# Slot products of an attention and soft-MoE kernel in eight wide matmuls, one reciprocal step per batch, and a new order of steps

## Chip, cores and metric

The kernel runs on one core of a Trainium2 chip. The metric is the device time of one execution in microseconds (us); lower is better. All data are float32. The engines are named as the profile names them: PE is TensorE (PEld its weight loads), DVE is VectorE, ACT is ScalarE, POOL is GpSimd, and SP issues the DMAs.

## What is computed

An attention between 512 tokens and 32 states per head, in both directions, feeds a soft mixture of experts over all 4608 rows (8 batches of 512 tokens and 32 states).

```python
# attention: x (8, 8, 512, 64), state (8, 8, 32, 64)
scores = scale * np.matmul(x, state.transpose(0, 1, 3, 2))      # softmax over the 32 states
xread = np.matmul(softmax(scores), state)
scores2 = scale * np.matmul(state, x.transpose(0, 1, 3, 2))     # softmax over the 512 tokens
sread = np.matmul(softmax(scores2), x)
x = concatenate([xread, sread], axis=2)                         # to (4608, 512)
# soft mixture of experts: phi (512, 32), w1 (8, 512, 1024), w2 (8, 1024, 512)
logits = x @ phi
d = np.exp(logits - logits.max(0)); d /= d.sum(0) + 1e-09       # over all rows
slot_input = d.T @ x                                            # 32 slots, 4 per expert
h = np.maximum(slot_input[e] @ w1[e], 0.0)
slot_out[e] = h @ w2[e]
c = np.exp(logits - logits.max(1)); c /= c.sum(1) + 1e-09       # over the 32 slots
return c @ slot_out
```

## The kernel before

The program is a list of small steps. The text `ORDER` names them one after the other, each with its batch, head parity or group, and each step issues its instructions when its turn comes; an engine takes its own instructions in that order and waits for what they need. A `!` behind a copy step puts that copy on DVE, without it the copy is on ACT. The text `HOMES` says by hand which of the 8 PSUM banks (`b`), 11 half buffers (`h`), 5 `big` and 8 `wide` buffers each new tile takes, so a tile also waits until the last user of its buffer is through.

Steps of batch b (h is the parity of the head, 0 or 1): `X` turns x on PE and `xe` copies it out. `S` makes the scores, two PSUM banks of 128x512, a row for each state of four heads. The token side of the softmax: `q` turns a bank with DVE (32x32 blocks), `m1` takes the largest of each 32, `sub` subtracts it on POOL, `x1` is the exponential on ACT, `l1` sums each 32 on DVE, `r1` adds the small constant and takes the reciprocal (two DVE instructions, lines 367 and 368), `mul` multiplies on POOL, and `aT` turns the result back on DVE. The state side: `m2` (DVE), `e2` (ACT, with the row sum), `l2` (two DVE instructions, lines 394 and 395), `E` and `ee` turn and copy the exponentials, `R` multiplies by x, `sr` divides, `srT` and `srTe` turn and copy.

The sums lie in `l1s` and `l2s` beside a column that holds 1e-9, so that one `tensor_reduce` over pairs adds the constant. `r1` runs for each h alone, so `mul.b.0` waits only for half 0.

`G` (line 291) makes the products of phi and the states once: for each of 8 batches and 4 head pairs one matmul with a 128x32 state as weights and a 64 columns wide `phi_bd`, in which POOL has laid phi out with zeros (lines 286 to 289). `Ge` copies the bank to `G_sb` on ACT (line 304). `Lx` multiplies `G_sb` with the turned softmax; this gives the logits without x ever being formed.

For a group of two batches then come the largest logit (`mx`, `mk`, `bm`, `nme`), `dx` (exponential), `dT` and `dTe` (turn and copy), `T` with the turned softmax `A` / `ae`, `tt` (DVE turn), `Px` with the turned states `U` / `Ue`, and `Y`, which adds to the running slot input `y`. `Ls` to `Ys` do the same for the rows of the states (`V` / `Ve` and `D` among them). `Wd`, `We`, `SI` and `SIe` close the softmax over all rows; `SIe` (line 728) writes the slot input `si_m`, on which all of the rest waits.

The rest: `W.hf.e` (line 755) multiplies with w1 into two halves, `hc`, `ht`, `hr` copy, turn and rectify a half into `h_m` (zeroed by `hz` on POOL), `u.c.hf.e` (line 817) multiplies with w2 into the two column halves c, `c` and `s` (lines 823 to 833) sum over the four row blocks, `cm`, `cx`, `cd`, `cb` make the softmax over the slots, `o.k.q` (line 842) makes 128x512 blocks of the output, four banks each, which ACT and DVE copy and SP sends out, and `os` does so for the state rows. For k = 3 each two copies are sent as a DMA of their own (`HALVED`).

SP issues all loads in one fixed order: x, states, phi, then 33.5 MB of weights, each as soon as its buffer is free (`ld`).

Of the kernel before, what the change touches and what calls it, by code (L numbers as in the profile page):

```python
# [32 lines left out]
X.0.0 xe.0.0! X.0.1 xe.0.1! X.0.2 X.0.3 xe.0.3 xe.0.2! S.0 q.0.0 X.1.0 xe.1.0 X.1.1 X.1.3 X.1.2 xe.1.1 m1.0.0  # L33
sub.0.0 m2.0.0 xe.1.3 xe.1.2 q.0.1 m2.0.1 m1.0.1 sub.0.1 x1.0.0 l1.0.0 r1.0.0 e2.0.1 G.0 Ge.0 S.1 q.1.0 X.2.3 E.0.1
mul.0.0 q.1.1 e2.0.0 x1.0.1 ee.0.1 l1.0.1 X.2.0 E.0.0 ee.0.0 X.2.1 X.2.2 m1.1.1 r1.0.1 xe.2.3 m1.1.0 xe.2.1 xe.2.0
sub.1.1 R.0.0 m2.1.0 aT.0.0 l2.0 m2.1.1 R.0.1 xe.2.2 S.2 e2.1.0 sub.1.0 x1.1.0 sr.0 m2.2.0 mul.0.1 aT.0.1 e2.1.1
x1.1.1 X.3.2 l2.1 E.1.0 ee.1.0 X.3.0 A.0.0 xe.3.0 ae.0.0 X.3.1 E.1.1 X.3.3 q.2.0 xe.3.1 srT.0 l1.1.1 q.2.1 ee.1.1
srTe.0 X.4.0 l1.1.0 m1.2.1 sub.2.1 r1.1.1 R.1.0 m2.2.1 xe.3.2 R.1.1 xe.3.3 S.3 sr.1 srT.1 r1.1.0 e2.2.0 E.2.0 e2.2.1
m1.2.0 X.4.2 x1.2.1 srTe.1 m2.3.0 ee.2.0 E.2.1 mul.1.1 aT.1.1 xe.4.0 X.4.1 ee.2.1 m2.3.1 mul.1.0 aT.1.0 sub.2.0
xe.4.1 A.1.1 X.4.3 Lx.0.0 Lx.0.1 l2.2 x1.2.0 Lx.1.0 Lx.1.1 ae.1.1 q.3.0 l1.2.1 ld.0 m1.3.0 sub.3.0 r1.2.1 mul.2.1  # L40
xe.4.3 R.2.0 R.2.1 xe.4.2 S.4 e2.3.0 mx.0 mk.0 sr.2 keep.0 srT.2 x1.3.0 bm.0 srTe.2 q.3.1 e2.3.1 A.0.1 l1.2.0 X.5.0
m1.3.1 sub.3.1 ae.0.1 r1.2.0 xe.5.0 m2.4.0 aT.2.1 X.5.3 xe.5.3 nme.0 X.5.2 q.4.0 mul.2.0 l1.3.0 dx.0 Lu.0 E.3.1
X.5.1 xe.5.2 m1.4.0 xe.5.1 E.3.0 r1.3.0 mul.3.0 A.1.0 sub.4.0 x1.3.1 dT.0 dTe.0 q.4.1 S.5 e2.4.0 U.0 l1.3.1 E.4.0
ae.1.0 T.0 ee.3.1 m1.4.1 ee.3.0 R.3.0 m2.4.1 R.3.1 e2.4.1 aT.2.0 A.2.0 l2.3 X.6.2 r1.3.1 ee.4.0 m2.5.0 mul.3.1
aT.3.0 A.3.0 Ue.0 x1.4.0 sr.3 srT.3 m2.5.1 aT.3.1 e2.5.0 xe.6.2 tt.0 sub.4.1 x1.4.1 X.6.1 E.5.0 Lx.2.0 Lx.2.1 q.5.0
l1.4.1 m1.5.0 sub.5.0 ae.2.0 Lx.3.0 srTe.3 r1.4.1 e2.5.1 l2.4 Lx.3.1 Ls.0 q.5.1 X.6.0 l1.4.0 E.4.1 m1.5.1 keep.1
Lse.0 mx.1 X.6.3 xe.6.1 r1.4.0 l2.5 A.2.1 X.7.1 ae.3.0 xe.6.0 xe.6.3 sub.5.1 S.6 x1.5.0 l1.5.0 A.3.1 q.6.1 ae.2.1
ee.4.1 ee.5.0 q.6.0 E.5.1 Lr.0 msx.0 mul.4.1 ae.3.1 R.4.0 R.5.0 R.4.1 ee.5.1 R.5.1 mk.1 pv.1 m1.6.1 m1.6.0 mul.4.0
m2.6.1 sr.4 x1.5.1 l1.5.1 bm.1 lkp.0 nme.1 xe.7.1 r1.5.0 aT.4.0 X.7.0 dsx.0 srT.4 e2.6.1 xe.7.0 dx.1 X.7.2 m2.6.0
E.6.1 xe.7.2 sub.6.0 aT.4.1 X.7.3 xe.7.3 sr.5 r1.5.1 mul.5.0 mul.5.1 dT.1 e2.6.0 sub.6.1 dTe.1 als.0 Lus.0 S.7 D.0  # L50
aT.5.0 ee.6.1 m2.7.1 aT.5.1 Px.0 V.0 E.6.0 ee.6.0 l2.6 x1.6.0 T.1 Lx.4.0 q.7.0 tt.1 al.0 m1.7.0 e2.7.1 srTe.4 x1.6.1
Ve.0 Lx.4.1 Lx.5.0 m2.7.0 e2.7.0 Lx.5.1 mx.2 R.6.0 R.6.1 srT.5 E.7.1 ee.7.1 A.5.1 E.7.0 sr.6 q.7.1 l1.6.0 m1.7.1
pv.2 mk.2 A.4.1 sub.7.0 srTe.5 ee.7.0 l1.6.1 x1.7.0 sub.7.1 ld.1 ld.2 ld.3 ae.5.1 srT.6 bm.2 nme.2 srTe.6 ae.4.1
r1.6.0 mul.6.0 l1.7.0 l2.7 Px.1 x1.7.1 keep.2 R.7.0 R.7.1 r1.6.1 A.4.0 A.5.0 sr.7 srT.7 dx.2 mul.6.1 srTe.7 ae.4.0
U.1 r1.7.0 Ps.0 Ls.1 Lse.1 l1.7.1 dT.2 dTe.2 aT.6.0 mul.7.0 A.6.0 r1.7.1 aT.6.1 Lr.1 ae.5.0 al.2 Lx.6.0 Lx.6.1 al.1
mul.7.1 aT.7.0 Ue.1 T.2 Lx.7.0 aT.7.1 msx.1 lkp.1! Lx.7.1 tt.2 ae.6.0 mx.3 pv.3! A.7.0 mk.3! Lu.1 als.1 A.6.1 dsx.1
Y.0 bm.3 D.1 Ys.0 nme.3 V.1 ae.7.0 A.7.1 Y.1 dx.3 dT.3 Px.2 Ve.1 ae.6.1! ld.4 ae.7.1! windows Lu.2 Ps.1 Y.2 Ys.1
dTe.3 T.3 Lus.1 al.3 Lu.3 tt.3 Wd Px.3 We Y.3 SI SIe W.0.0 W.0.1 ld.5 ld.6 keep.3! cm.1 hz W.0.2 W.0.3 W.0.4 W.0.5
W.0.6 W.0.7 W.1.0 hc.0 ht.0 cm.0 W.1.1 W.1.2 cm.2 cx.2 hr.0 u.0.0.0 W.1.3 u.0.0.1 W.1.4 u.0.0.2 W.1.5 ld.7 ld.8 ld.9
ld.10 u.0.0.3 ld.11 W.1.6 cx.0 cd.0 u.1.0.0 W.1.7 cx.1 cd.1 u.0.0.4 u.0.0.5 hc.1! ht.1 u.0.0.6 u.0.0.7 hr.1 u.0.1.0  # L60
u.0.1.1 ld.12 u.0.1.2 u.0.1.3 u.0.1.4 ld.13 ld.14 cd.2 cb.2 cb.1 u.0.1.5 u.0.1.6 u.0.1.7 ld.15 u.1.1.0 c.0 s.0
u.1.0.1 cb.0 o.1.0 os.0 o.1.1 o.0.0 o.0.1 u.1.1.1 u.1.0.2 u.1.1.2 u.1.0.3 u.1.1.3 u.1.0.4 u.1.1.4 u.1.0.5 u.1.1.5
# [4 lines left out]
0 1 2 3 4 0 2 3 4 1 0 2 3 4 1  # L67
# [859 lines left out]
```

## Time and profile before

| what | value |
|---|---|
| median of 3 runs | 136.93 us (136.19 to 139.18) |
| the profiled execution's own time | 135.94 us |
| its span, first to last instruction | 134.1 us |
| PE busy | 116.4 us (87%) |
| DVE busy | 89.9 us (67%) |
| ACT busy | 74.5 us (56%) |
| POOL busy | 45.1 us (34%) |
| HBM read, written | 42.53 MB, 8.91 MB |

Times inside the execution count from the start of the span. Busy time is a sum over instructions; the ends of matmuls are modelled, so a PE that reads as busy may still have room.

### The profile page before, as it was taken

The numbers are of one execution on the slowest core, as the hardware profiler recorded it, in microseconds if no ns is written. First come the engines' busy times: TensorE is split into PE (matmuls) and PEld (weight loads), VectorE is DVE, ScalarE is ACT, GpSimd is POOL, SyncE is SP. The second block draws the span as 40 slices with busy tenths as digits, with TensorE's granted clock in tenths as the row PEclk, the third lists the DMA queues.
The fourth block names the chain that finished last, engine by engine and source line by source line (L and its number), as shares of the span: only waits on it lengthen the run. The fifth ranks groups of instructions, "written<-read, shape, count | busy, mean of one in ns | idle before, by whom it ended". The sixth has DMA issues, their size and how long they took to land.

```text
span 134.1 us, 4428 instructions
## 1 busy us (share of the span) xinstructions
PE 116.4 (87%) x1852; PEld 80.1 (60%) x1852; DVE 89.9 (67%) x228; ACT 74.5 (56%) x179; POOL 45.1 (34%) x64
## 2 busy tenths in 40 slices
...
GB/s 115 370 412 452 415 440 401 450 420 432 428 415 445 410 445 398 428 423 447 418 435 406 414 394 345 420 430 442 423 440 392 57 348 434 418 134 338 419 428 147
DMA packets 7220, 51.73 MB, mean 386 GB/s; under 512 B 800, under 2 KB 928, under 8 KB 3488
## 3 DMA queue, kind: packets, MB, share of 16 engines
...
q14 instruction: 6, 0.05, 0.1%
HBM read 42.53 MB, written 8.91 MB: 384 GB/s over the span
## 4 chain that ended last, share of the span: by engine, by line
PE 62%; DVE 19%; issue 5%; DMA 5%; ACT 1%; DVEq 0%; SPq 0%; ACTq 0%
PE h_ps L755 11%; PE o L842 7%; PE xt_ps L320 7%; PE so_ps L817 6%; DMA out_x<-out 5%; PE an_ps L402 4%; PE sc L334 4%; PE sr_ps L427 4%; PE spin L282 3%; DVE nm L383 3%; PE eT_ps L402 3%; DVE aT L377 3%; DVE m L352 3%; DVE q L347 3%; PE lt L457 2%
## 5 line engine op out<-in xcount | busy, mean ns | idle before, releaser
L356 POOL TENSOR_TENSOR q<-q,m 128x512 f32<-128x512 f32 x16 | 16.7, 1048 | 19.5 <-DVE r L367 11.2
L261 ACT ACTIVATE xt<-xt_ps 128x512 f32<-128x512 f32 x29 | 16.5, 619 | 6.9 <-PE xt_ps L320 6.8
L372 POOL TENSOR_TENSOR q<-q,r 128x512 f32<-128x512 f32 x16 | 16.7, 1049 | 6.1 <-DVE r L368 3.3
L854 DVE COPY out<-o 128x512 f32<-128x512 f32 x16 | 10.0, 683 | 12.1 <-PE o L842 12.0
L320 PE MATMUL xt_ps<-ident,x 128*128 128x128 f32 x112 | 16.3, 276 | 0.0
L755 PE MATMUL h_ps<-w,si_m 128*32 128x512 f32 x128 | 15.3, 594 | 0.4 <-DVE si_m L728 0.4
L320 PEld LDWEIGHTS xt_ps<-ident,x 128*128 128x128 f32 x112 | 12.6, 141 | 3.1 <-issue 2.7
L817 PE MATMUL so_ps<-w,h_m 128*32 128x256 f32 x216 | 14.2, 380 | 0.0
L817 PEld LDWEIGHTS so_ps<-w,h_m 128*32 128x32 f32 x216 | 8.2, 110 | 7.2 <-issue 4.3
L258 ACT COPY so_sb<-so_ps 128x256 f32<-128x256 f32 x2 | 0.7, 372 | 19.9 <-PE so_ps L817 14.2
L347 DVE STREAM_TRANSPOSE q<-sc 128x512 f32<-128x512 f32 x16 | 10.9, 693 | 1.2 <-PE sc L334 1.2
L388 ACT ACTIVATE e<-sc,nm 128x512 f32<-128x512 f32 x16 | 11.2, 700 | 0.6 <-DVE nm L383 0.4
L842 PE MATMUL o<-lt_all,so_r 32*128 32x512 f32 x64 | 10.8, 630 | 0.5 <-ACT so_r L258 0.5
L377 DVE STREAM_TRANSPOSE aT<-q 128x512 f32<-128x512 f32 x16 | 11.0, 690 | 0.3 <-PE sc L334 0.2
L853 ACT COPY out<-o 128x512 f32<-128x512 f32 x16 | 8.7, 591 | 3.8 <-PE o L842 3.6
L383 DVE TENSOR_REDUCE nm<-sc 128x1 f32<-128x512 f32 x16 | 10.6, 661 | 0.0
L352 DVE TENSOR_REDUCE m<-q 128x16 f32<-128x512 f32 x16 | 10.6, 665 | 0.0
L363 DVE TENSOR_REDUCE l1s<-q 128x16 f32<-128x512 f32 x16 | 10.4, 649 | 0.0
L359 ACT ACTIVATE q<-q 128x512 f32<-128x512 f32 x16 | 10.2, 634 | 0.2 <-POOL q L356 0.2
L755 PEld LDWEIGHTS h_ps<-w,si_m 128*32 128x32 f32 x128 | 8.6, 110 | 2.6 <-issue 0.8
L334 PE MATMUL sc<-xt,x_b 64*32 64x512 f32 x112 | 9.8, 601 | 0.2 <-ACT xt L261 0.2
L258 ACT COPY eT<-eT_ps 128x512 f32<-128x512 f32 x16 | 9.2, 600 | 1.2 <-PE eT_ps L402 1.2
...
## 6 DMA issues: line engine op xcount, KB each, us to landing
...
```

What stands on the lines that cost most here:

```text
L261: (dve.tensor_scalar_mul if Z["dve"] else act.mul)(out, in_, by)
L320: pe.transpose(p[:, P * j : P * j + P], xg[b, g][:, j, :], ident)
L334: pe.matmul(r[f"sp{h}"][32 * g : 32 * g + 32, :], st_t(b, g)[64 * h : 64 * h + 64, :], r[f"xt{g}"][64 * h : 64 * h + 64, :], start=True, s ...
L347: dve.transpose(r[f"q{h}"], r[f"sp{h}"])
L352: dve.tensor_reduce(out=r[f"m1{h}"], in_=r[f"qv{h}"], axis=AX.X, op=ALU.max)
L356: pool.tensor_tensor(v, v, R[b][f"m1{h}"].broadcast_to([P, 16, NS]), op=ALU.subtract)
L372: pool.tensor_tensor(v, v, R[b][f"r1{h}"].broadcast_to([P, 16, NS]), op=ALU.mult)
L377: dve.transpose(r[f"aT{h}"], r[f"q{h}"])
L383: dve.tensor_reduce(out=r[f"nm2{h}"], in_=r[f"sp{h}"], axis=AX.X, op=ALU.max, negate=True)
L755: pe.matmul(h_ps[hf][32 * kt : 32 * kt + 32, :], si_m[kt // 2][:, 256 * (kt % 2) + 32 * e : 256 * (kt % 2) + 32 * e + 32], wt[1, hf, e, kt ...
L817: pe.matmul(so[c][32 * i : 32 * i + 32, :], h_m[hf][:, 256 * i + 32 * e : 256 * i + 32 * e + 32], wt[2, c, e, 4 * hf + i], start=i0, stop= ...
L842: pe.matmul(o[j], so_r[hf][rows, col : col + 128], lt_all[rows, 4 * q : 4 * q + 4, :].rearrange("p b s -> p (b s)"), start=True, stop=True,)
```

## The change

The products of phi and the states become 8 matmuls of 256 columns: phi is now the weight, 64 rows and 32 columns of it, and the states of all 8 batches are streamed; two banks result, which two DVE transposes turn into `G_sb`, and `phi_bd` goes. `l1s` and `l2s` become one tile `ls` with 34 pairs per batch (two times 16 of the token side, 2 of the state side), and `r1` (twice) and `l2` become one step `rr` of one reduction and one reciprocal over 34 numbers. It stands behind both `l1` and both `e2` of its batch; `mul` and `sr` read their part of it. `ORDER` and `HOMES` are replaced.

```diff
-    l1s = cp.tile([P, 4, 16, 2], F32, name="l1s")
-    l2s = cp.tile([P, 2, 2, 2], F32, name="l2s")
-    pool.memset(l1s, EPS)
-    pool.memset(l2s, EPS)
+    ls = cp.tile([P, 2, 34, 2], F32, name="ls")
+    pool.memset(ls, EPS)
...
-        phi_bd = half("phi_bd")[:, 0 : 8 * NS].rearrange("p (g h n) -> p g h n", g=4, h=2)
-        pool.memset(phi_bd, 0.0)
-        for h in range(2):
-            pool.tensor_copy(phi_bd[64 * h : 64 * h + 64, :, h, :], phi_sb[64 * h : 64 * h + 64])
...
         def G(b):
-            R[0]["gp"] = p = bank([P, B, 2 * NS], "g_ps")
-            for b in range(B):
-                for g in range(4):
+            p = R[0]["gp"] = [bank([P, B * NS], f"g_ps{h}") for h in range(2)]
+            for g in range(4):
+                for h in range(2):
                     pe.matmul(
-                        p[32 * g : 32 * g + 32, b, :],
-                        st_t(b, g),
-                        phi_bd[:, g].rearrange("p h n -> p (h n)"),
+                        p[h][32 * g : 32 * g + 32, :].rearrange("p (q b n) -> p q b n", q=4, b=2),
+                        phi_sb[64 * h : 64 * h + 64, g, :],
+                        stT_sb[64 * h : 64 * h + 64, :, g % 2, g // 2],
...
-            act.copy(G_sb, R[0]["gp"].rearrange("p b (h n) -> p b h n", h=2))
+            for h in range(2):
+                dve.transpose(G_sb[:, h].rearrange("p b n -> p (b n)"), R[0]["gp"][h])
...
-        def r1(b, h):
-            R[b][f"r1{h}"] = t = sm.tile([P, 16, 1], F32, tag=f"r1{h}", name=f"r1_{b}_{h}")
-            dve.tensor_reduce(out=t, in_=l1s[:, 2 * (b % 2) + h], axis=AX.X, op=ALU.add)
+        def rr(b):
+            R[b]["rr"] = t = sm.tile([P, 34, 1], F32, tag="rr", name=f"rr_{b}")
+            dve.tensor_reduce(out=t, in_=ls[:, b % 2], axis=AX.X, op=ALU.add)
             dve.reciprocal(t, t)
...
-        def l2(b):
-            R[b]["l2"] = t = sm.tile([P, 2, 1], F32, tag="l2", name=f"l2_{b}")
-            dve.tensor_reduce(out=t, in_=l2s[:, b % 2], axis=AX.X, op=ALU.add)
-            dve.reciprocal(t, t)
...
-u.1.0.6 u.1.1.6 u.1.0.7 u.1.1.7 c.1 s.1 o.2.0 o.3.0 o.3.1 spin.3 o.2.1 os.1
+u.1.0.6 u.1.1.6 u.1.0.7 u.1.1.7 c.1! s.1! o.3.0 o.3.1 os.1 o.2.0 o.2.1 spin.3
```

On DVE before there are, in the attention, three `xe`, two `ae`, and one each of `keep`, `lkp`, `mk` and `pv`; now three `xe`, three `ae`, two `lkp`, and one each of `srTe`, `dTe` and `Ve`. After the attention DVE had `hc.1`; now it has `hc.0`, `c.0`, `c.1` and `s.1`.

Three places show how the order moves. The first is DVE in batches 2 and 3 (the first number in a name is the batch, the second the half). Before:

```order
L352 TENSOR_REDUCE m_3_0_610<-q_0_605 128x16
L367 TENSOR_REDUCE r_2_1_613<-l1s 128x16
L368 RECIPROCAL r_2_1_613<-r_2_1_613 128x16
L473 TENSOR_REDUCE mx_666<-lt_582 128x1
L438 TENSOR_TENSOR sr_670<-sr_ps_619,l_2_591 128x128
L347 STREAM_TRANSPOSE q_1_679<-sc_1_509 128x512
L363 TENSOR_REDUCE l1s<-q_0_444 128x16
L352 TENSOR_REDUCE m_3_1_694<-q_1_679 128x16
L367 TENSOR_REDUCE r_2_0_698<-l1s 128x16
L368 RECIPROCAL r_2_0_698<-r_2_0_698 128x16
```

Now, for the same batch 2:

```order
L345 TENSOR_REDUCE m_3_0_604<-q_0_594 128x16
L340 STREAM_TRANSPOSE q_1_640<-sc_1_439 128x512
L345 TENSOR_REDUCE m_3_1_642<-q_1_640 128x16
L355 TENSOR_REDUCE ls<-q_0_503 128x16
L255 COPY srT_455<-srT_ps_626 128x4x32
L361 TENSOR_REDUCE rr_664<-ls 128x34
L362 RECIPROCAL rr_664<-rr_664 128x34
L426 TENSOR_TENSOR sr_680<-sr_ps_514,rr_664 128x128
```

Half 1 had its reciprocal three large steps ahead of half 0; now both halves and the state side have theirs in one step, behind the last sum.

The second place is DVE at the end of the attention, from the last group's `nme.3` to `SIe`. Before:

```order
L537 TENSOR_REDUCE nm_all<-bm_ps_1573 128x1
L529 SCALAR_TENSOR_TENSOR y<-y,al_all,px_ps_1388 128x128
L258 COPY an_1549<-an_ps_1_1564 128x16x32
L258 COPY an_1584<-an_ps_1_1586 128x16x32
L529 SCALAR_TENSOR_TENSOR y<-y,al_all,px_ps_1598 128x128
L529 SCALAR_TENSOR_TENSOR y<-y,al_all,ps_ps_1619 128x128
L585 STREAM_TRANSPOSE tt_1650<-t_ps_1628 128x128
L700 TENSOR_SCALAR rl<-l_ps 128x32
L701 RECIPROCAL rl<-rl 128x32
L529 SCALAR_TENSOR_TENSOR y<-y,al_all,px_ps_1654 128x128
L728 TENSOR_TENSOR si_m_1613<-si_ps,rl 128x8x4 x2
L728 TENSOR_TENSOR si_m_1615<-si_ps,rl 128x8x4 x2
```

Now; behind these rows follow three `y`, the two `rl` and the four `si_m`:

```order
L525 TENSOR_REDUCE nm_all<-bm_ps_1464 128x1
L255 COPY an_1421<-an_ps_1_1458 128x16x32
L255 COPY an_1489<-an_ps_0_1467 128x16x32
L255 COPY an_1489<-an_ps_1_1473 128x16x32
L637 TENSOR_REDUCE lr_1494<-lr_1494 128x1
L493 TENSOR_TENSOR nm_all<-lr_1494,nm_all 128x1
L517 SCALAR_TENSOR_TENSOR y<-y,al_all,px_ps_1500 128x128
L573 STREAM_TRANSPOSE tt_1517<-t_ps_1393 128x128
L517 SCALAR_TENSOR_TENSOR y<-y,al_all,ps_ps_1512 128x128
L255 COPY srN_1520<-v_ps_1448 128x512
L658 STREAM_TRANSPOSE D_1525<-ds_1522 128x32
L573 STREAM_TRANSPOSE tt_1570<-t_ps_1527 128x128
```

More of DVE's work stands behind `nme.3` (the row of `nm_all`) than before: the state group's part, a third `an`, a copy of `srN` and a second `tt` have moved there.

The third place is PE between the last product of the first column half (`so_ps` of c = 0) and the first output block. Before:

```order
L817 MATMUL so_ps_1752<-w_1789,h_m 32x256 x4
L817 MATMUL so_ps_1808<-w_1791,h_m 32x256 x4
L832 MATMUL sum_ps_1904<-so_sb_1901,rep 128x256
L817 MATMUL so_ps_1808<-w_1797,h_m 32x256 x4
L842 MATMUL o_0_0_1912<-lt_all,so_r_1903 128x512
```

Now:

```order
L805 MATMUL so_ps_1730<-w_1647,h_m 32x256 x4
L805 MATMUL so_ps_1817<-w_1657,h_m 32x256 x8
L820 MATMUL sum_ps_1827<-so_sb_1813,rep 128x256
L805 MATMUL so_ps_1817<-w_1676,h_m 32x256 x8
L830 MATMUL o_0_0_1840<-lt_all,so_r_1826 128x512
```

In both, `so_sb` is the copy of the first bank. Before, one part of the second half stood between that bank and the sum (its fellow far ahead, in the w1 stage), now two; behind the sum two instead of one.

## Rows read from the trace of the kernel before

**Rows 1.** By stage: stretch, length, busy PE, PEld, DVE, ACT, POOL, clock, DMA, GB/s

```profile
5.30:54.80 49.50, 48.29 (x905) 36.65 (x905) 46.84 (x113) 44.36 (x107) 26.07 (x29) 1.00 1.01 423
54.80:79.30 24.50, 20.56 (x474) 16.75 (x473) 19.55 (x61) 16.21 (x46) 11.00 (x20) 1.00 1.01 422
79.30:102.80 23.50, 23.50 (x280) 15.53 (x280) 11.75 (x33) 1.94 (x4) 7.08 (x7) 1.00 1.01 414
102.80:110.50 7.70, 7.62 (x52) 3.31 (x46) 4.54 (x8) 5.26 (x11) 0.00 (x0) 1.00 0.55 225
...
117.60:124.50 6.90, 5.64 (x39) 2.44 (x39) 4.88 (x8) 4.74 (x10) 0.00 (x0) 1.00 0.57 236
```

**Rows 2.** Chain that ended last: start us, us, what; one l2, one r1

```profile
28.40 0.05 DVE l L394
28.47 0.17 DVE l L395
...
30.41 0.10 DVE r L367
30.54 0.25 DVE r L368
```

**Rows 3.** Groups by form: sums and reciprocals on DVE (busy us, mean ns)

```profile
L368 DVE RECIPROCAL r<-r 128x16 f32<-128x16 f32 x16 | 4.0, 253 | 0.6
L367 DVE TENSOR_REDUCE r<-l1s 128x16 f32<-128x32 f32 x16 | 2.8, 172 | 0.0
L395 DVE RECIPROCAL l<-l 128x2 f32<-128x2 f32 x8 | 1.3, 166 | 0.3
L394 DVE TENSOR_REDUCE l<-l2s 128x2 f32<-128x4 f32 x8 | 0.9, 113 | 0.0
L701 DVE RECIPROCAL rl<-rl 128x32 f32<-128x32 f32 x1 | 0.4, 353 | 0.0
```

**Rows 4.** The same chain: G and the scores of the next batch

```profile
10.97 1.03 PE g_ps L295 x64
12.00 1.02 PE sc L334 x16
```

**Rows 5.** Groups by form: the copy of G, and a DVE transpose of 256 columns

```profile
L304 ACT COPY G_sb<-g_ps 128x512 f32<-128x512 f32 x1 | 0.6, 576 | 0.0
L791 DVE STREAM_TRANSPOSE c<-lts_all 128x256 f32<-128x256 f32 x1 | 0.4, 434 | 0.0
```

**Rows 6.** Groups by form: DVE's copies of the output

```profile
L854 DVE COPY out<-o 128x512 f32<-128x512 f32 x16 | 10.0, 683 | 12.1 <-PE o L842 12.0
```

**Rows 7.** Waits: engine line <- releaser: us in total, times, longest us

```profile
POOL q L356 <- DVE r L367: 11.2, 5, 4.5
PEld t_ps L574 <- ACT st L258: 1.3, 1, 1.3
```

**Rows 8.** Timeline of DVE: the last group's largest logit, and the slot input

```profile
74.28 0.16 DVE L537 TENSOR_REDUCE nm_all<-bm_ps 128x1 f32<-128x5 f32 x1
...
79.03 0.48 DVE L728 TENSOR_TENSOR si_m<-si_ps,rl 128x32 f32<-128x32 f32 x4 [0.49 <-PE si_ps L710]
```

**Rows 9.** The same view: DVE's last stretch of the attention

```profile
74.28:79.51 5.23, 4.22 (x88) 3.14 (x89) 3.99 (x16) 1.61 (x5) 0.38 (x2) 1.00 1.01 405
```

**Rows 10.** Timeline of PE after the attention: two waits, and one run of u

```profile
98.84 2.04 PEld L817 LDWEIGHTS so_ps<-w,h_m 128*32 128x32 f32 x39 [0.48 <-DVE h_m L777]
...
103.25 0.30 PEld L832 LDWEIGHTS sum_ps<-so_sb,rep 128*128 128x128 f32 x2 [0.57 <-ACT so_sb L258]
...
110.55 5.39 PE L817 MATMUL so_ps<-w,h_m 128*32 128x256 f32 x96
```

**Rows 11.** Groups by form: steps of the token side around the reciprocal

```profile
L372 POOL TENSOR_TENSOR q<-q,r 128x512 f32<-128x512 f32 x16 | 16.7, 1049 | 6.1 <-DVE r L368 3.3 <-ACT eT L258 1.5 <-DVE D L670 1.3
L363 DVE TENSOR_REDUCE l1s<-q 128x16 f32<-128x512 f32 x16 | 10.4, 649 | 0.0
L359 ACT ACTIVATE q<-q 128x512 f32<-128x512 f32 x16 | 10.2, 634 | 0.2 <-POOL q L356 0.2
```

More of the change, by code (lines that the diff above doesn't have):

```diff
@@ L32 @@
 ORDER = """
[L33 to L62, printed above, removed]
@@ new lines @@
+xe.3.0 xe.3.1 X.3.2 E.1.1 q.2.1 srT.0 xe.3.2 sub.1.1 m2.2.1 X.4.2 ee.1.1 x1.1.1 S.3 l1.1.0 e2.2.1 e2.2.0 m1.2.1
+srTe.0 R.1.1 X.4.1 E.2.1 l1.1.1 aT.0.0 rr.1 xe.4.1 E.2.0 X.4.0 ee.2.1 q.2.0 A.0.0 m2.3.0 ee.2.0 R.2.0 sub.2.1
+mul.0.1 aT.0.1 e2.3.0 R.2.1 x1.2.1 mul.1.0 aT.1.0 A.1.0 m2.3.1 mul.1.1 aT.1.1 ae.0.0 Lx.0.0 xe.4.0 Lx.0.1 Lx.1.0
+sr.1 m1.2.0 ae.1.0 Lx.1.1 q.3.0 l1.2.1 mx.0 E.3.0 m1.3.0 e2.3.1 xe.4.2 ee.3.0 X.4.3 xe.4.3 sub.2.0 x1.2.0 A.0.1
+srT.1 ae.0.1 X.5.3 A.1.1 ae.1.1 q.3.1 m1.3.1 l1.2.0 sub.3.0 E.3.1 sub.3.1 ee.3.1 X.5.2 xe.5.2 mk.0 srTe.1! rr.2 S.4
@@ new lines @@
+mul.2.0 bm.0 sr.2 srT.2 X.5.1 q.4.0 x1.3.1 l1.3.1 nme.0 x1.3.0 l1.3.0 aT.2.0 keep.0 rr.3 R.3.0 R.3.1 m2.4.0 xe.5.1
+q.4.1 dx.0 xe.5.3 m2.4.1 mul.2.1 aT.2.1 X.5.0 xe.5.0 mul.3.0 sr.3 m1.4.1 srTe.2 dT.0 dTe.0 m1.4.0 X.6.1 S.5 q.5.1
+mul.3.1 T.0 e2.4.0 E.4.0 sub.4.1 xe.6.1 aT.3.1 X.6.2 pv.1 srT.3 tt.0 e2.4.1 E.4.1 X.6.0 srTe.3 A.2.0 xe.6.2 x1.4.1
+ee.4.1 sub.4.0 A.2.1 aT.3.0 m2.5.1 x1.4.0 X.6.3 ae.2.0 l1.4.0 Lx.2.0 m1.5.1 sub.5.1 Lx.2.1 l1.4.1 Lx.3.0 Lx.3.1
+ee.4.0 R.4.0 rr.4 q.5.0 mul.4.0 ae.2.1 Ls.0 R.4.1 m2.5.0 xe.6.0 keep.1 sr.4 A.3.0 e2.5.1 E.5.1 mx.1 xe.6.3 m1.5.0
```

46 lines of the change are left out of this document (33 added, 13 removed), and 8 rows, old and new, of the table b.

## Prediction

> **What bounds the kernel now.** I read the busy time by stage first. In the attention's first stage, 5.3 to 54.8 us, DVE is busy 46.84 of 49.50 us (95%), ACT 44.36 and PE 48.29, whose ends are modelled; DVE has the least room [rows 1]. In the second, 54.8 to 79.3, DVE falls to 19.55 of 24.50 (80%) and PE to 20.56: dependences cost more there than any one engine. From 79.3 to 102.8 PE is busy all the time with w1 and half of w2, and DVE half of it. Beside all this the DMA runs at a share of 1.00 and 414 to 423 GB/s up to 102.8, which is the load of the weights; only then does its share drop, to 0.55 and, between the output's two halves, to 0.57. So there are two clocks in this kernel. The loads can't come much sooner, but nothing on PE waits for them to 102.8, and the idle of the DMA behind it is time in which outputs weren't ready. Whatever makes the attention end sooner moves the outputs forward by as much until the first of them meets the end of the loads. That is about 3.5 us, the 0.45 of 7.70 us without transfers in the row of 102.80 to 110.50.
>
> I read the chain of waits next, for the price of a step from one start to the next; the group's mean holds the part that overlaps its successor. Then the waits, the groups by form, and the timeline of the last stretches.
>
> **The merged sums and reciprocals.** Before, a batch has two `r1` and one `l2`. By the starts in the chain an `r1` takes 0.13 + 0.25 = 0.38 us and an `l2` 0.07 + 0.17 = 0.24 [rows 2], together 1.00 us a batch. The new step isn't in the trace. From 16 to 32 numbers the reciprocal grows from 253 to 353 ns, 6.25 ns each, so 34 take 253 + 18 x 6.25 = 366 ns [rows 3]. The reduction grows from 113 ns for 4 inputs to 172 for 32, 2.1 ns each, so 68 take 172 + 36 x 2.1 = 248, or 0.20 us from start to start by the 0.13 of the smaller one. Together 0.57 us, a saving of 0.43 a batch. Bounds: nothing, if the time goes by numbers alone, and 0.62, if the wide step costs what one `r1` does. I take 0.43, since it lies on two measured slopes. Six of the eight steps stand before the last batch's scores, that is in the stage that DVE bounds: 2.6 us off it.
>
> There the rows tell of a cost per instruction: 2 numbers still take 166 ns and 4 inputs 113 [rows 3]. The Trainium skill, Perfetto Trace Analysis, section on optimizing Scalar and DVE operations, puts the overhead of one DVE instruction on SBUF at about 60 ns and advises larger operations where the engine is saturated. The 48 instructions become 16, so by that rule alone an estimated 32 x 0.06 = 1.9 us go instead of 8 x 0.43 = 3.4, and the forecast below would be about 1.2 us higher; the intercepts in the rows are larger, and I go by them.
>
> **G.** 64 matmul records take 1.03 us; the next scores, 16 records of 512 columns with the same 64-row and 32-column tiles that G now uses, take 1.02 [rows 4]. Half the columns make about 0.5, so PE saves 0.5 us once. But the copy was 576 ns on ACT and becomes two DVE transposes of 434 ns [rows 5], some 0.8 us from start to start. Bounds for PE are 0 and 1.0. POOL loses its three instructions for `phi_bd`, ahead of the first `sub`; I count nothing for them. In the stage that DVE bounds, G costs +0.8.
>
> **Copies moved to DVE.** In the first stage one `srTe` and one `lkp` more, 128 columns each: DVE copies 512 in 683 ns [rows 6], so under 0.3 each, +0.5 together. First stage: -2.6 + 0.8 + 0.5 = **-1.3 us**. ACT is relieved by G's 0.58 and those two, so it doesn't take DVE's place. Bounds: -2.4 (0.62 a batch) and +1.3 (0).
>
> **The end of the attention.** Here the merged steps save 2 x 0.43, and a third `an`, a `srN` and a `dT` copy come to DVE while one `keep` leaves; that cancels. What counts is order. (a) PE's weight load for a `t_ps` waits 1.3 us, put down to ACT's copy `st` [rows 7]; that copy stood just ahead of this `T`, and now stands far behind it, for its only reader is a later `Px`: -1.0. (b) From the start of the last group's `nme` to the end of `SIe` are 79.03 + 0.48 - 74.28 = 5.2 us [rows 8], of which DVE is busy 3.99 [rows 9]. By the order it now has two more copies of 512 columns there (the third `an`, and `srN`) at 0.68 [rows 6], and one `y`, one `tt`, the state group's maximum and `D`, an estimate of 1.0 together by the prices of short steps in [rows 3]: 3.99 + 1.36 + 1.0 = 6.3 us, and few holes, since it comes from different chains. So that stretch grows by 1.1. (c) The 2.4 us of DVE work that moved into it no longer stand ahead of `nme.3`. DVE idles a fifth there and other chains take part of the room; I take under half, -0.9. Together **-0.8 us**. Bounds: -2.3 (all three in full, -1.0 + 1.1 - 2.4) and +1.1 ((b) alone).
>
> **After the attention.** PE's work is the same. Two waits go: 0.48 us for `h_m`, since all eight parts of u on the first half of h now stand between the last w1 part and the second half's, instead of two, then `ht`, then two; and 0.57 for `so_sb`, since two parts of u stand there instead of one [rows 10]. A part is 8 records, 96 in 5.39 us, 0.45 each, so two cover 0.9 us of DVE's copy: **-1.0**. `hz` now stands late on POOL, behind `cd.1`'s multiplication, but w1's 16 parts give it time. Then the second column half: the first block sent was a whole one (four copies), now it is one of those sent by halves, so its first DMA leaves one pair of copies, 0.68 us, sooner [rows 6], into a DMA that idles [rows 1]; the transfers behind it are the same bytes: **-0.5**, as c = 1's two copies on DVE give 0.1 back. Bounds of these two: -1.7 and -0.4.
>
> **Loads.** They stay in their order on SP. Buffers: the `big` ones for w2 now follow w1's parts 0 to 3 instead of 1 to 4, so no later. At 422 GB/s nothing is won or lost.
>
> **Sum.** -1.3 - 0.8 - 1.0 - 0.5 = -3.6 us. The profiled execution took 135.94 (span 134.1 and 1.8 around it), so 132.3 for its like; the median of the runs is 0.99 above it, and on that the forecast is **133.3 us**. A measurement of this kernel can tell about 2%, 2.7 us.
>
> **Rivals.** *DVE's relief is not on the path.* ACT at 90% and PE at 98% by its rows stand close behind DVE in the first stage [rows 1]; if these wait for each other in turn, a shorter DVE only waits more. The first stage then gives 0.4, the end of the attention nothing, the rest 1.0: 135.5 us. For it speaks that all three are so full; against it that the chain of waits lies on DVE through that stage, in the very steps that shrink [rows 2].
>
> *The joint step starves POOL.* `mul` of the first half now also waits for the second half's exponential and sum, 0.634 + 0.649 = 1.28 us [rows 11], and for both `e2`. POOL takes its work in order, so behind a waiting `mul` stand the `sub` of a later batch, behind that ACT's `x1`, behind that DVE's `l1` of the next batch. If this is open in a batch, the batch costs 1.28 us. Three such batches eat the gain; from five on, 6.4 - 3.6 = 2.8, the change is slower by 2%: 139.7 us. For it: POOL's `sub` already waits 11.2 us for `r` in all [rows 7]. Against it: POOL works only 26.07 of 49.50 us in the first stage [rows 1], and the new order puts other batches' `sub` ahead of several `mul`.
>
> *The end of the attention closes up fully.* The moved work leaves no hole ahead of `nme.3`, so (c) counts in full: -2.3 there instead of -0.8, 131.8 us. For it: DVE's 4.95 us of idle time in that stage [rows 1]. Against it: the waits there are many and short, and a chain of `mx`, `mk`, `bm`, `nme` that no order shortens ends it.
>
> **Chances.** The forecast 0.46, with its own range 132.2 to 134.6; relief off the path 0.30; the end closing up 0.14; POOL starved 0.10. The forecast's part beyond 134.2 us (2% under the median) I put at 0.06, and a fifth of the last rival stays within 2%. Faster by over 2%: 0.40 + 0.14 = 0.54; within 2%: 0.06 + 0.30 + 0.02 = 0.38; slower: 0.08. The bounds added up reach from 130.5 to 138.9; leaving out a tenth on each side I give 131.0 to 136.8.
>
> **What would show it.** Right: about 0.57 us for each `rr` pair from start to start; the scores of batch 7 about 1.3 us sooner than 54.8; `SIe` about 2 us sooner than 79.5; no wait of PE for `h_m` and for the first `so_sb`; a DMA share above 0.55 in the first gap, with the first output sooner by 3 us. Wrong: POOL's waits for the reciprocal above 20 us, or ACT's for POOL growing, with DVE's idle time in the first stage above its 2.7 us; an `SIe` at 79 or later; PE waiting for weights before 102 us; or the first gap of the DMA unchanged.

## The result, and the profile after

The changed kernel takes 133.15 us in the median (4 runs, 131.94 to 134.4), the kernel before 136.73 on the same chip: ratio 0.9675, 95% interval 0.9606 to 0.9743. It is faster. The ratio is that of the fast runs alone (131.94 and 132.27 us against 136.19 to 136.93), since two of the changed kernel's four runs and one of the other's lie over 1.5% above the fastest. Measured twice more it gave 0.9678 (0.9643 to 0.9714) and 0.9744 (0.9668 to 0.9820). The profiled execution took 132.27 us with a span of 130.5, against 135.94 and 134.1. So 3.6 us of the span went, as the forecast's sum said, but not all of them where it said.

The stretches of [rows 1] in the changed kernel, with the same columns; behind them DVE's first stage from 10.00 us on, and the attention up to the end of `SIe`.

```profile
5.30:54.80 49.50, 47.79 (x868) 36.45 (x867) 45.45 (x91) 43.35 (x103) 24.09 (x24) 1.00 1.01 423
54.80:79.30 24.50, 22.60 (x484) 17.56 (x486) 22.27 (x61) 15.42 (x47) 12.44 (x23) 1.00 1.01 421
102.80:110.50 7.70, 7.70 (x84) 4.03 (x81) 5.30 (x9) 4.61 (x9) 0.00 (x0) 1.00 0.81 338
110.50:117.60 7.10, 5.94 (x75) 2.75 (x66) 2.32 (x5) 1.51 (x4) 0.00 (x0) 1.00 0.78 319
117.60:124.50 6.90, 3.01 (x19) 1.38 (x19) 3.74 (x7) 3.06 (x7) 0.00 (x0) 0.87 1.02 418
10.00:54.80 44.80, 43.41 (x831) 33.31 (x829) 44.06 (x89) 41.67 (x100) 23.74 (x23) 1.00 1.01 427
5.30:77.25 71.95, 68.34 (x1331) 52.10 (x1332) 65.70 (x147) 58.77 (x149) 36.19 (x46) 1.00 1.01 423
```

The rows of before for the last two stretches:

```profile
10.00:54.80 44.80, 43.59 (x865) 33.41 (x864) 44.14 (x109) 43.45 (x106) 25.47 (x27) 1.00 1.01 427
5.30:79.51 74.21, 69.06 (x1379) 53.61 (x1381) 66.60 (x175) 60.57 (x152) 37.06 (x49) 1.00 1.01 423
```

DVE's work up to `SIe` shrinks by only 0.9 us (66.60 to 65.70), but its idle time shrinks too, from 7.61 to 6.25. And the second stage, where DVE was busy 19.55 of 24.50 us [rows 1], now has 22.27: most holes there have closed (its last 2 us are w1 by now). The gap in the DMA is smaller (a share of 0.81 instead of 0.55).

The chain of waits (start us, us, what), with one `rr`, the scores of batch 7 and the start of w1:

```profile
34.40 0.14 DVE rr L361
34.57 0.38 DVE rr L362
34.97 0.29 DVE sr L426
...
55.33 1.09 PE sc L327 x16
...
77.05 8.20 PE h_ps L743 x72
```

This `rr` takes 34.97 - 34.40 = 0.57 us from start to start. But the scores of batch 7, at 54.8 before, are half a microsecond later, although w1 (79.28 before) is 2.2 sooner.

The groups that answer [rows 3, 5], then the waits that answer [rows 7]:

```profile
L362 DVE RECIPROCAL rr<-rr 128x34 f32<-128x34 f32 x8 | 2.9, 367 | 0.3
L361 DVE TENSOR_REDUCE rr<-ls 128x34 f32<-128x68 f32 x8 | 1.7, 211 | 0.1
L297 DVE STREAM_TRANSPOSE G_sb<-g_ps 128x256 f32<-128x256 f32 x2 | 0.7, 408 | 0.0
```

```profile
POOL q L349 <- DVE m L345: 22.0, 10, 7.5
POOL q L366 <- DVE rr L362: 1.8, 3, 1.3
```

POOL's product `mul` waits for the reciprocal 1.8 us in all, against 3.3 before [rows 11]. The 11.2 us of [rows 7] don't belong beside them: `sub` reads `m` and not `r`, and by the timeline of DVE an `m` had ended just ahead of each `r` named there (ends 23.96 and 24.05 us, for one, and `sub` starts at 24.13). So those were waits for `m` already. They have grown, to 22.0 us: POOL is ahead of DVE. The timeline of DVE gives the ends of the last stretch, as [rows 8], and that of PE and SP the tail, as [rows 10]:

```profile
70.56 0.16 DVE L525 TENSOR_REDUCE nm_all<-bm_ps 128x1 f32<-128x5 f32 x1 [0.58 <-PE bm_ps L480]
...
76.80 0.48 DVE L716 TENSOR_TENSOR si_m<-si_ps,rl 128x32 f32<-128x32 f32 x4
```

```profile
100.41 0.30 PEld L820 LDWEIGHTS sum_ps<-so_sb,rep 128*128 128x128 f32 x2 [0.41 <-DVE so_sb L255]
...
104.60 4.08 SPq L847 DMA_DIRECT2D out_x<-out  x4
116.89 2.76 SPq L845 DMA_DIRECT2D out_x<-out  x4
```

`nme.3` is 3.7 us sooner, `SIe` 2.2. The first output goes out at 104.60 (107.00 before), 2.4 us sooner where 3 were forecast.

### The profile page after: what moved, and what is told of

It reads as the page before. It is cut to its first block, busy times and chain, and to the rows that moved or that the text cites. A ratio compares the mean times of both kernels' runs of the same rounds, so it can differ in the third digit from the quotient of the medians.

```text
span 130.5 us, 4299 instructions
## 1 busy us (share of the span) xinstructions
PE 114.8 (88%) x1804; PEld 77.2 (59%) x1804; DVE 90.0 (69%) x203; ACT 71.9 (55%) x173; POOL 44.3 (34%) x60
## 4 chain that ended last, share of the span: by engine, by line
PE 65%; DVE 17%; DMA 5%; issue 2%; ACT 2%; SPq 1%; DVEq 1%; ACTq 0%
PE h_ps L743 11%; PE so_ps L805 11%; PE xt_ps L313 7%; PE sc L327 6%; PE eT_ps L390 5%; DMA x<-x_in 5%; PE o L830 5%; PE sr_ps L415 4%; PE an_ps L390 4%; DVE ls L355 3%; DVE aT L371 3%; PE t_ps L562 3%; DVE out L842 3%; PE lt L445 2%; DVE m L345 1%
## 5 line engine op out<-in xcount | busy, mean ns | idle before, releaser
L366 POOL TENSOR_TENSOR q<-q,rr 128x512 f32<-128x512 f32 x16 | 16.4, 1048 | 4.1 <-DVE rr L362 1.8
L743 PE MATMUL h_ps<-w,si_m 128*32 128x512 f32 x128 | 14.4, 594 | 0.5 <-DVE si_m L716 0.5
L805 PE MATMUL so_ps<-w,h_m 128*32 128x256 f32 x216 | 12.8, 381 | 0.0
L382 ACT ACTIVATE e<-sc,nm 128x512 f32<-128x512 f32 x16 | 11.2, 706 | 2.0 <-DVE nm L377 1.2
L355 DVE TENSOR_REDUCE ls<-q 128x16 f32<-128x512 f32 x16 | 10.5, 668 | 0.0
L390 PE MATMUL an_ps<-ident,aT 128*128 128x128 f32 x64 | 9.4, 277 | 1.1 <-DVE aT L371 0.7
L830 PE MATMUL o<-lt_all,so_r 32*128 32x512 f32 x64 | 9.8, 624 | 0.5 <-DVE so_r L255 0.5
L390 PE MATMUL eT_ps<-ident,e 128*128 128x128 f32 x64 | 10.0, 281 | 0.1
L805 PEld LDWEIGHTS so_ps<-w,h_m 128*32 128x32 f32 x216 | 6.7, 110 | 5.4 <-issue 1.1
```

Source lines behind the costliest of these rows:

```text
L355: dve.tensor_reduce(out=ls[:, b % 2, 16 * h : 16 * h + 16, 0:1], in_=R[b][f"qv{h}"], axis=AX.X, op=ALU.add)
L366: pool.tensor_tensor(v, v, R[b]["rr"][:, 16 * h : 16 * h + 16].broadcast_to([P, 16, NS]), op=ALU.mult)
L390: pe.transpose(p[:, j, :], r[f"{src}{h}"][:, P * j : P * j + P], ident)
L743: pe.matmul(h_ps[hf][32 * kt : 32 * kt + 32, :], si_m[kt // 2][:, 256 * (kt % 2) + 32 * e : 256 * (kt % 2) + 32 * e + 32], wt[1, hf, e, kt ...
L805: pe.matmul(so[c][32 * i : 32 * i + 32, :], h_m[hf][:, 256 * i + 32 * e : 256 * i + 32 * e + 32], wt[2, c, e, 4 * hf + i], start=i0, stop= ...
L830: pe.matmul(o[j], so_r[hf][rows, col : col + 128], lt_all[rows, 4 * q : 4 * q + 4, :].rearrange("p b s -> p (b s)"), start=True, stop=True,)
```

## What the page had shown and the forecast passed over

The page of the kernel before gives "issue" 5% of the chain that ended last: time in which an engine waited for nothing that the profile shows. The timeline of PE has the longest of it in three places, in the middle of groups of equal matmuls, where nothing could be waited for:

```profile
51.72 0.48 PE L427 MATMUL sr_ps<-x,eT 128*32 128x64 f32 x20 [0.69 <-issue]
65.26 0.30 PE L608 MATMUL px_ps<-st,tt 64*32 64x64 f32 x3 [1.73 <-issue]
71.41 0.27 PE L457 MATMUL lt<-aT,G_sb 128*32 128x128 f32 x1 [1.02 <-issue]
```

The page also lists a DMA queue "q8 instruction" with 14 packets and 0.23 MB, 16 KB each, about as many as PE has blocks of 256 instructions (3737 in all). Counting PE's instructions from the first, the stops fall 256 instructions, or a multiple of that, apart from each other. The windows from the start of one such block to the next (columns as above: of the two numbers in brackets for PE and PEld, the sum is 252 to 256):

```profile
51.72:58.98 7.26, 7.08 (x126) 5.56 (x127) 6.97 (x21) 6.08 (x18) 4.49 (x6) 1.00 0.99 416
58.98:65.26 6.28, 4.55 (x128) 4.29 (x128) 5.49 (x16) 5.84 (x17) 2.48 (x3) 1.00 1.04 437
65.26:71.41 6.15, 5.13 (x127) 4.20 (x127) 4.78 (x14) 3.74 (x12) 4.61 (x8) 1.00 1.01 428
71.41:77.20 5.79, 5.79 (x126) 4.89 (x126) 3.88 (x13) 3.24 (x10) 1.52 (x7) 1.00 0.97 407
```

The DMA view of 62.9 to 64.0 us, within PE's stop of 63.53 to 65.26, has one packet of instructions; by the trace's records it ran from 62.98 to 63.91:

```profile
q1 hardware_dynamic: 39, 0.46, 100.6%
q8 instruction: 1, 0.02, 5.3%
```

Every one of the five blocks that begin from 51.72 to 77.20 was entered 1.28 to 1.43 us after its packet had ended, and its packet began 2.6 to 4.9 us after PE had entered the block before. The starts of these blocks are 4.9 (46.86 to 51.72) to 7.3 us apart, whatever is in them. I read from this that from 51.7 us to the end of the attention the supply of PE's instructions paced the kernel before; the run with 96 idle instructions below tests it. The changed kernel has no such stop. In its three profiles the blocks of that stage are entered 1.6 us or more behind their packets, and PE has 96 instructions less: G's 64 records with 64 weight loads became 16 with 16.

The Trainium skill (Runtime: NRT & Kernel Launch, section on instruction fetch mechanics) says that an engine's instructions are fetched in blocks of 16 KiB, 256 instructions, through a DMA queue of its own. The traces agree for PE: packets of 16 KB, and stops 256 instructions apart. It also calls the cost of a block's end mostly hidden; here PE stood still for up to 1.73 us at one, and the measurement decides.

The expectations of theories 1 and 2 below were written without this.

## Experiments

Theory 1 is the forecast's: the shorter sums are on the path. Theory 2 is its rival: what pays is the order, and DVE's relief is not on the path. Theories 3 and 4 came later. Beside the ratios I use one measure from the profiles: from PE's first product for the scores of batch 0 to the start of `SIe`. It leaves out when x lands. In three profiles of the changed kernel it is 68.03 (76.80 - 8.77), 68.30 and 68.03 us, 68.1 in the mean; before, 79.03 - 7.27 = 71.76. Between the two orders it doesn't compare: the old one puts the first scores ahead of `X.1.0`, and the changed kernel with that place for them (a run below) has 76.41 - 7.07 = 69.34. So I hold each run against the kernel with its own order. Line numbers differ by a few between the kernels; `lt`, line 445 in the changed one, keeps its name.

**The changed kernel again, twice.** No edit.

> The changed kernel once more, on the same chip as the three variants of it. 132.3 us in its profiled execution again, SIe's first instruction at 76.8 us of the span, by every theory; it is what the others are held against.

> The changed kernel again, as the measure of this call: 132.3 us in the like of its profiled execution.

Measured: ratios 0.9678 and 0.9744, as above.

**The merged step taken apart**, in the new order.

```diff
-... rr.0 ...
+... r1.0.0 r1.0.1 l2.0 ...
```

> The changed kernel with the joint step taken apart: at the place of each rr stand the two r1 and the l2 of the kernel before, the half whose product comes first ahead. Theory 1, DVE bounds the attention and the merged steps are what relieves it: each batch pays 1.00 instead of 0.60 us on DVE, 3.2 us in all; SIe comes 2 to 3 us later than in the changed kernel and the time rises by as much, to 134.3 to 135.3. Theory 2, the order alone made the gain and the merged steps lie beside the path: SIe moves by less than 0.7 us and the time with it. If the wait of the products for the whole batch cost something, the split step would even win up to 1 us.

Measured: 0.9969 (0.9929 to 1.0008); first scores to `SIe` 80.29 - 8.90 = 71.39, so +3.3 us. Without the merged steps the change gains nothing that can be told. Eight times the 0.43 us of the forecast are 3.4: the steps count in full. The timeline of PE has the scores of batch 7 at 57.57 us:

```profile
57.57 1.09 PE L335 MATMUL sc<-xt,x_b 64*32 64x512 f32 x16
```

That is 48.67 us after the first scores, against 55.33 - 8.77 = 46.56 in the changed kernel: 2.1 of the 3.3 us are lost by then. Theory 2 falls.

**The old G in the new order.**

```diff
-            for h in range(2):
-                dve.transpose(G_sb[:, h].rearrange("p b n -> p (b n)"), R[0]["gp"][h])
+            act.copy(G_sb, R[0]["gp"].rearrange("p b (h n) -> p b h n", h=2))
```

(with its 32 narrow matmuls and `phi_bd`)

> The changed kernel with G as before: 64 matmuls of 64 columns on phi_bd, which lies in a still unused part of lt_all, and one copy on ACT. Theory 1 (DVE bounds): DVE is rid of two transposes of 0.41 us, so SIe comes 0.3 to 0.7 us sooner though PE pays 0.4 more. Theory 2 (PE's order bounds the start): PE's 0.4 us come through and SIe is 0.2 to 0.5 us later. If neither is on the path, no change within 0.2.

Measured: 0.9840 (0.9789 to 0.9891); to `SIe` 78.16 - 8.41 = 69.75, +1.6 us, more than either theory had. 0.75 us of it is lost by the scores of batch 7 (55.72 - 8.41 = 47.31). DVE is busy less, 42.86 of the 44.80 us from 10.00 on, and the kernel is slower: not DVE's time is what the new G saves. The timeline of PE shows one reason for the rest, in the middle of a group again:

```profile
69.98 0.43 PE L450 MATMUL lt<-aT,G_sb 128*32 128x128 f32 x8 [0.78 <-issue]
```

**`X.1.0` behind the first scores**, since it waits for x to land.

```diff
-... X.0.3 X.1.0 xe.0.3! S.0 ...
+... X.0.3 xe.0.3! S.0 X.1.0 ...
```

> The changed kernel with X.1.0 (the first turn of batch 1, whose load lands at about 8.1 us) behind S.0 instead of ahead of it. Scores of batch 0 should end at 9.2 to 9.4 instead of 9.9 us and DVE's first maximum start at about 9.4 instead of 10.0. Theory 1 (DVE bounds from there on): SIe comes 0.4 to 0.7 us sooner, time 0.3 to 0.5% lower. Rival: the half us is lost again in DVE's later holes, SIe within 0.2 us.

Measured: 0.9699 (0.9652 to 0.9746), and `SIe` starts at 76.41 (76.58 in the run beside it without the edit). The scores of batch 0 do start at 7.07 instead of 8.28, but those of batch 7 only at

```profile
54.94 1.09 PE L332 MATMUL sc<-xt,x_b 64*32 64x512 f32 x16
```

instead of 55.11. The wait for x is worth 0.2 us; the rival holds.

**The last outputs in the old order.**

```diff
-... s.1! o.3.0 o.3.1 os.1 o.2.0 o.2.1 spin.3
+... s.1! o.2.0 o.3.0 o.3.1 spin.3 o.2.1 os.1
```

> The changed kernel with the order of the last output steps as before: o.2.0, o.3.0, o.3.1, spin.3, o.2.1, os.1, so that the first block sent is a whole one of 1 MB. By the forecast's term the first DMA of the second half leaves one pair of copies later, 0.6 us, and the end moves by as much: 132.9 in the like of the profiled execution. Rival: the end hangs on the last block's copies and its own 1 MB transfer, which come sooner here, so nothing or a small gain.

Measured: 0.9749 (0.9702 to 0.9796), beside 0.9744 for the changed kernel measured with it: no difference in the ratios. In the profiles the second half's first DMA goes 117.08 - 76.41 = 40.67 us after `SIe` starts, against 116.89 - 76.80 = 40.09, so 0.58 sooner in the changed kernel; the term of 0.5 is of that size, but too small for the ratios.

**The old attention with the new rest.**

```diff
-... Wd SI We SIe W.0.0 lkp.1! ...
+... Wd Px.3 We Y.3 SI SIe W.0.0 keep.3! ...
```

(all up to `SIe` as before, all behind it as changed)

> The kernel before up to SIe, and behind it the changed kernel's order of the w1, w2 and output steps, with buffers assigned to fit. If the two parts of the change are independent, SIe stays at 79.0 us and the time is lower than before by the terms behind the attention alone, 1.4 to 1.5 us: 134.5 in the like of 135.94. Rival: the loads or buffers fit the new attention only and PE waits for weights; then the gain is under 0.7.

Measured: 0.9915 (0.9874 to 0.9957), or 1.2 us of the 3.6; PE's stops in the attention are those of before (0.8, 1.6 and 1.0). The forecast had 1.5 for this part.

**The joint step in the old order**: the two `r1` of a batch become one, and the products that stood between them move behind it.

```diff
-... r1.2.1 mul.2.1 ... r1.2.0 ... mul.2.0
+... r1.2 mul.2.1 ... mul.2.0
```

> The kernel before with the two r1 of each batch in one step (32 numbers) at the place of the later one, and a product that stood ahead of it moved right behind it; the rest of the order as it was. By the rival of the prediction, POOL and what stands behind it starve, and the time is 1 to 4 us above before though DVE does 8 x 0.25 = 2 us less. By theory 1 without it, DVE's 2 us come through in part: 1 to 2 us below before. If the gain needs the new order, no change within 0.7 us.

Measured: 1.0197 (1.0148 to 1.0246); to `SIe` 81.89 - 7.40 = 74.49, +2.7 us. Waits of POOL and DVE in it:

```profile
POOL q L361 <- DVE m L357: 9.8, 7, 2.1
POOL q L361 <- PE sr_ps L433: 4.1, 1, 4.1
POOL q L378 <- DVE r L374: 3.8, 3, 2.9
DVE aT L383 <- POOL q L378: 4.7, 6, 1.2
```

and DVE in its first stage:

```profile
10.00:54.80 44.80, 40.85 (x814) 30.59 (x811) 41.21 (x91) 40.98 (x99) 23.57 (x26) 1.00 1.01 427
```

DVE had less to do and was busy only 41.21 us of 44.80: its `aT` waits 4.7 us for POOL's product, a wait that the kernel before doesn't have. This is the rival "the joint step starves POOL", true in the old order and not in the new one.

For the last four runs, theory 3 says that PE's instruction supply is the second limit, and that where the blocks end in the work decides; theory 4, that G was worth only the engines' time. The 6.2 us that theory 3 takes for a block is near the middle of what was seen (4.9 to 7.3), not a floor.

**96 idle instructions more on PE**, beside its warm-up.

```diff
-        for j, n in ((4, 128), (4, 128), (3, 64)):
+        for j, n in ((4, 128), (3, 64)):
...
+        for i in range(24):
+            pe.matmul(spin[32 * (i % 4) : 32 * (i % 4) + 32, 0:32], y[:, 0:32], y[:, 0:32], start=True, stop=True)
```

> The changed kernel with 24 calls of 32 columns on PE beside its warm-up, in place of one of the warm-up's calls: 48 records of matmuls and 48 weight loads, 96 instructions more on PE, done before x has landed, with no reader and no other work. Theory 3, instruction supply: PE's instructions come in blocks of 256 (16 KB packets of the instruction queue), a block can't be entered earlier than some 6.2 us after the one before it, and the kernel before has four such blocks in a row up to the end of its attention, with PE's stops of 0.69, 1.73 and 1.02 us inside groups; the 96 fewer instructions of G took them away. Then these 96 put the blocks' ends back where the kernel with the old G had them: PE stops of 0.5 us or more inside a group, the largest close to 70 us, the end of SIe 0.7 to 1.6 us later than 76.4 to 76.9, ratio to the kernel before 0.974 to 0.982. Theory 4, G was worth its PE, ACT and POOL time: nothing changes, end of SIe within 0.4 us, ratio 0.967 to 0.972.

Measured: 0.9821 (0.9738 to 0.9904); to `SIe` 79.68 - 9.67 = 70.01, +1.9 us, of which only 0.25 are lost by the scores of batch 7 (56.48 - 9.67 = 46.81). No work was added behind 5 us, but PE stops where theory 3 puts it:

```profile
71.51 0.53 PE L447 MATMUL lt<-aT,G_sb 128*32 128x128 f32 x11 [1.34 <-issue]
```

PE's first products of x also took longer with the shorter warm-up (12 records in 2.79 us, 2.11 in the changed kernel), which the measure leaves out and the ratio does not. The profiled execution was the longest of the four (135.14 us, the others 133.12 to 134.6), so the 1.9 us may be too many. The ratio's interval lies above theory 4's range (0.9738 against 0.972) but overlaps that of the changed kernel's third measurement. What tells is the stop of 1.34 us, which the changed kernel has in none of its profiles.

**256 of them.** The same with `range(64)`, and no other warm-up.

> The same with 64 calls in place of the whole warm-up: 128 records and 128 weight loads, 256 instructions, one whole block. Theory 3: the ends of the blocks stand at the same places of the work as in the changed kernel, so although there are more instructions than with 96, there are no stops of PE inside groups behind 12 us, and the time is that of the changed kernel, 0.967 to 0.973, but for what the first products of x start later (each such us counts in full). If the cost goes by the number of instructions alone, it is slower than the run with 96. Theory 4: as the changed kernel too, but then the run with 96 is as well.

Measured: 0.9856 (0.9815 to 0.9897); to `SIe` 79.06 - 10.21 = 68.85, +0.7 us. More instructions than above cost less up to `SIe`, and no group on PE is cut by a stop of half a microsecond, which speaks for the place of the blocks' ends and not the number; the two ratios can't be told apart. But theory 3 expected nothing here, and 0.7 us are left: from 43.30 us on five blocks in a row were entered 1.20 to 1.43 us behind their packets, as in the kernel before, so PE was still at the end of its supply.

**The wide G cut in four**: each call split by columns, 64 records again, but turned by DVE.

```diff
+                    for q in range(4):
...
-                        stT_sb[64 * h : 64 * h + 64, :, g % 2, g // 2],
+                            stT_sb[64 * h : 64 * h + 64, q, g % 2, g // 2],
```

> The changed kernel with each of G's 8 wide calls cut into 4 of 64 columns: 64 records in place of 16, 96 PE instructions more, still turned by DVE, no phi_bd on POOL and no copy on ACT. Theory 3: most of what the old G cost comes back, the end of SIe 0.8 to 1.6 us later, a PE stop inside a group near 70 us, ratio 0.975 to 0.983. Theory 4: only PE's 0.4 us more beside G, end of SIe 0 to 0.5 later, ratio 0.967 to 0.974.

Measured: 0.9929 (0.9888 to 0.9971); to `SIe` 79.51 - 9.06 = 70.45, +2.3 us, slower than either expected, with PE's stop in `lt` again:

```profile
71.33 0.53 PE L446 MATMUL lt<-aT,G_sb 128*32 128x128 f32 x12 [0.78 <-issue]
```

But 1.35 of the 2.3 us are lost by the scores of batch 7 (56.97 - 9.06 = 47.91 against 46.56), and these are not supply alone: both theories had the cost of G itself on PE too small. The chains have it at

```profile
13.13 2.11 PE g_ps L288 x62
...
12.95 0.64 PE g_ps L287 x14
...
12.80 1.03 PE g_ps L293 x64
```

in this run, in the changed kernel and in the one with the old G. The same columns in four times the records take some 1.4 us more of PE. So this run gives no price for the supply, and none for DVE's two transposes (0.7 us in the group above) against the old G.

**The wide G alone, in the old order.**

```diff
-            act.copy(G_sb, R[0]["gp"].rearrange("p b (h n) -> p b h n", h=2))
+            for h in range(2):
+                dve.transpose(G_sb[:, h].rearrange("p b n -> p (b n)"), R[0]["gp"][h])
```

> The kernel before, in its old order, with G in the new form alone (8 wide calls, two transposes on DVE, no phi_bd, no ACT copy). Theory 3: 96 instructions less are 96/256 of a block, 0.375 x 6.2 = 2.3 us of supply in the stretch that it bounds; the stops inside px (1.73) and lt (1.02) go or move, the end of SIe is 0.7 to 2.3 us sooner than 79.5 although DVE has two transposes more, ratio 0.983 to 0.995. Theory 4, and the forecast's term of +0.8 for G: 0.995 to 1.006, with the stops as they were.

Measured: 1.0169 (1.0085 to 1.0253); to `SIe` 81.44 - 7.72 = 73.72, +2.0 us. Both theories missed the time. The stops did move, as theory 3 alone says, but the end of a block now fell among the turns of x for batch 7. The timeline of PE, with the scores of batch 6 first:

```profile
47.93 1.37 PE L337 MATMUL sc<-xt,x_b 64*32 64x512 f32 x16
...
56.76 0.55 PE L323 MATMUL xt_ps<-ident,x 128*128 128x128 f32 x3 [1.76 <-issue]
57.14 0.38 PE L563 MATMUL dT_ps<-ident,dx 128*128 128x128 f32 x2
57.45 2.46 PE L337 MATMUL sc<-xt,x_b 64*32 64x512 f32 x16
```

and one of its windows, with the granted clock as the third number from the end:

```profile
58.00:60.00 2.00, 2.00 (x31) 1.17 (x20) 0.58 (x1) 1.60 (x5) 1.38 (x3) 0.50 1.01 426
```

PE stood for 1.76 us, DVE ran dry (busy 0.58 of these 2.00 us), and the granted clock fell from 1.00 to 0.50 (1.2 of 2.4 GHz); the scores took 2.46 us where those of the batch before took 1.37. The clock seems the smaller part of it: two more executions of this program, with a mean clock of 0.97 instead of 0.96, took 137.82 and 137.95 us, 0.4 to 0.5 less than the profiled one.

No version tried beats the changed kernel.

## Why the prediction was right, and where its steps failed

The sum was -3.6 and the span lost 3.6. By the steps:

- **The merged sums.** 0.57 us a pair was forecast and is measured (reciprocal 366 against 367 ns, reduction 248 against 211). All eight count in full: 3.3 us come back when they are split.
- **First stage, -1.3.** This step failed. The scores of batch 7 were to come 1.3 us sooner and came 0.5 later. The shorter sums do pay there, 2.1 us by the run that splits them and not 2.6: five `rr` and not six have started by then, the sixth starts at 55.78 us. Something else in the new order takes them back and more. With the sums split, batch 7's scores are 57.57 - 54.81 = 2.8 us later than before; the forecast's 1.3 for G and the copies is not enough for that, and by the next point G costs nothing. The later start on x is 0.2 of it. Which of the moved steps costs the rest stays open; the forecast had put the move itself at nothing there.
- **G, +0.8 within it.** Failed in sign. DVE pays its 0.7, but with the old G the kernel is 1.6 us slower, 0.75 of it by batch 7's scores and the rest behind them, where PE then stops for 0.78. The forecast gave the shorter time on PE (0.64 instead of 1.03 us in the chain) no weight, since it held DVE for the only limit of that stage, and it counted columns and not instructions.
- **End of the attention, -0.8.** Failed in size: with the first stage's 0.5 us of delay to make up for, this stage gained 2.7. (b) was 76.80 + 0.48 - 70.56 = 6.7 us instead of 6.3. (c) was far too small: from the scores of batch 7 to `nme.3` the change gained 4.2 us, and (a) and (c) had 1.9. The `keep` that was set against three new copies stood behind `SIe` before, so it left nothing there. The step saw DVE idle a fifth of that stage and called it dependences; in that stage of before, PE's stops alone are 0.69 (up to 51.72, just ahead of it), 1.73 and 1.02 us. PE's wait behind `st` for `t_ps` (a) is gone, from 1.3 us, and the longest that `t_ps` now has is 0.8 behind `dT`.
- **The two together.** -2.2 us was measured up to w1 and -2.1 forecast. That the sum is right is luck: two failures of about 1.8 us cancel.
- **After the attention, -1.0.** Held: from w1's start to the first output block of the second column half it is 37.88 us instead of 38.74, -0.9. The wait for `h_m` is gone; that for `so_sb` is only down from 0.57 to 0.41, since the second part covers less of the copy than I took.
- **Output halves, -0.5.** Held: from that block's start to the half's first DMA 1.96 us instead of 2.55, -0.6.
- **Rivals.** Relief off the path fell with the run that splits the step. POOL starved fell for the changed kernel, but holds in the old order. The end closing up was nearest to what happened in that stage, though for another reason.

The parts do not add up. In the old order the joint step costs 2.7 us and the wide G 2.0; in the new order undoing them costs 3.3 and 1.6, together more than twice the 2.2 us by which `SIe` comes sooner. So each pays in the new order only. How much the order is worth by itself, with neither part, was not tried.
